# A hand-ordered list of operations is reordered: table load first, watches spread, count cast earlier

## The chip, the cores and the metric

The kernel runs on one core of a Trainium2 chip. The time is device microseconds of one execution, from which the median of three runs is shown; the profile is that of a further execution, with its own time. Engines: PE (TensorE: products), DVE (VectorE), ACT (ScalarE), POOL (GpSimd) and SP (SyncE, which only issues transfers here). Each engine works through its own list in order; a wait in it holds up all that is behind it.

## The reference

Two parts in a row. The first is a linear recurrence with complex gates, per batch (4), head (8) and step (768), with 48 x 48 states; the second is a feed-forward block with a squared ReLU on the 3072 tokens of 384 features that the first yields.

```python
mag = np.sqrt(a_re * a_re + a_im * a_im)
scale = np.minimum(mag, 0.999) / (mag + 1e-06)
a_re_n, a_im_n = (a_re * scale, a_im * scale)
for t in range(S):
    ar, ai = (a_re_n[:, :, t, :, None], a_im_n[:, :, t, :, None])
    new_re = ar * S_re - ai * S_im
    new_im = ar * S_im + ai * S_re
    S_re, S_im = (new_re + k_t * v_t, new_im)      # outer product
    y[:, :, t] = q_t @ S_re
x = y.transpose(0, 2, 1, 3).reshape(3072, 384)
h = np.maximum(x @ w_in, 0.0)                      # w_in 384 x 2048
out = h * h @ w_out                                # w_out 2048 x 384
```

The weights come as 8-byte floats and are decoded to 4-byte floats on the chip.

## The kernel before, in words

The tokens are worked in 12 groups (number gi) of two chunks (b = 0, 1) of 128 steps of one sequence each. For a group, the recurrence is turned into products of queries and keys that carry running products of the gates ("operands"), a masked score product per chunk, and a carried state. The feed-forward block then runs on the 256 tokens of the group.

The order of everything is written out by hand: FRONT is one string of tokens, `follow` walks through it and calls for each token the function that issues its instructions, and `manual_schedule` keeps that order on all five engines. The order of two tokens matters only if they have instructions on the same engine. Waits between engines and for transfers follow from the data. The tokens:

- l, i: loads of raw (the inputs of a group; l on SP's queue, ScalarE's and some on POOL, i on POOL for the first groups), v: values, f, j: transfers of words (a block of weights; f on SP, j on POOL). raw is one buffer for all groups.
- p0.k, q0.k: step k of the operands of group 0, chunk 0 and chunk 1; p1, q1: those of group 1; o2.k to o11.k: of later groups, both chunks at once. Steps 0 to 2, 4 to 6, 8 to 10, 12, 14, 18 and 22 are ScalarE's; 3, 7, 11, 13, 15, 16, 19, 20 and 23 to 30 VectorE's (of p0.9, too). 15, 23, 24, 25, 16, 26, 27 are seven steps that build running products in blocks (`steps_in_blocks`, two instructions each), 17 is the scan of the blocks' totals (`totals`, line 918: on POOL for group 0, on VectorE else), 18 copies it (`carries`, line 937), 19 multiplies it in (`carried`), 20, 28, 29, 30 are the four products of queries and keys, 21 two small transfers on SP (line 968).
- a, b: chunk 0 and 1 of a group: .0 scores, .1 and .3 keys transposed, .2 and .4 copied, .5 masked (VectorE), .6 values summed (line 1059), .7 tokens copied to x (line 1071, ScalarE), .8 the state's product (line 1084), .9 the new state. g: gap transfers within x (line 1129, SP), without which no product can start.
- U, S, A: the decoding of a block of words: two casts on ScalarE (lines 666, 674) and one operation on VectorE (line 682). A0 to A7 are the blocks of w_in, A8 to A15 of w_out.
- F, H: a part of the first product (groups 0 and 1 by chunk: line 1137, 24 records each; others line 1153, 12 records each) and the squared ReLU behind it (two ACTIVATEs). h_ps has two buffers. T, E: the second product of groups 0 and 1 (line 1173) and its eviction (line 1116). Z, X, Y, Q, R: the second product of the later groups in seven half products of 16 records (line 1243), the sums on VectorE that they need, and the output's parts (R: lines 1116, 1119). s: stores on SP.
- I: keep_busy, two products of an identity into an unused PSUM tile (four records each, line 579), which compute nothing.
- M: constants. M9 makes ident and the seed of the mask on POOL, M1 the mask: two copies on ScalarE (line 611), a transpose on TensorE (line 614), two copies on ScalarE (line 617). M0 is a small ACTIVATE with the function that p0.4 and q0.4 use, into a place that is overwritten later.
- w, W: the range check reads the weights a second time: w is a transfer of 384 KB into a single buffer (line 694), W two short ACTIVATEs on it (lines 704, 705). K0 compares what was gathered, K1 sums it over partitions on TensorE (line 1372), K2 casts the count (line 1375). All engines then load the count (line 1456) and branch past a second path that serves other inputs (line 1457); with these inputs it isn't taken.

Before, M0 stands behind p0.2, M9 ahead of i0.1.1, M1 behind p0.18, sixteen I's ahead of M1; most w and W stand in the second half, K0 ahead of Z11.4 and K1, K2 behind the last product.

Of the kernel before, what the change touches and what calls it, by code (L numbers as in the profile page):

```python
# [23 lines left out]
I32 = mybir.dt.int32  # L24
I16 = mybir.dt.int16
U32 = mybir.dt.uint32
U8 = mybir.dt.uint8
F8 = mybir.dt.float8e5
# [401 lines left out]
def quotient_path(ctx, tc, feat, vtok, w_in, w_out, w1, w2, out, n_seq, count):  # L430
# [816 lines left out]
    def outputs(i, r):  # L1247
# [242 lines left out]
```

## Time and profile before

| | us |
|---|---|
| median of 3 runs (lowest, highest) | 651.23 (650.91, 651.72) |
| profiled execution: time, span | 649.98, 648.2 |
| PE busy, DVE busy, ACT busy, POOL busy | 614.3, 480.2, 431.9, 72.9 |
| mean granted clock of TensorE | 0.988 of full speed |

The span is from the first to the last instruction of the profiled execution; its own time is 1.8 us longer. A busy PE is modelled and includes waiting of pipelined products, so its idle time says more than its busy time. The trace has all 6467 products of the program.

### The profile page before, as it was taken

The page shows a single profiled execution, that of the slowest core. Times are in us where ns is not written, and L with a number is a line of the kernel's source. Part 1 is how long each engine was busy: PE and PEld are TensorE (multiplying, and loading weights), DVE is VectorE, ACT ScalarE, POOL GpSimd, SP SyncE. Part 2 cuts the span into 40 slices and gives each one's busy share as a digit, 9 for nine tenths or more (in the row PEclk, how much of TensorE's full clock was granted, in tenths as well). Part 3 has the DMA queues.
Part 4 walks back from the last instruction along what each step waited for, and adds up shares of the span by engine and source line. Part 5 has one row for each costly group of instructions (what it writes and reads, how often), then busy time and mean ns, then how long its engine had stood idle before and what let it go on. Part 6 is the DMA issues. An engine that isn't in the chain of part 4 may idle for free.

```text
span 648.2 us, 15843 instructions
## 1 busy us (share of the span) xinstructions
PE 614.3 (95%) x6467; PEld 552.2 (85%) x6467; DVE 480.2 (74%) x937; ACT 431.9 (67%) x848; POOL 72.9 (11%) x154
## 2 busy tenths in 40 slices
PE   3389999999999999999999999999999999999994
PEld 3389977686899889889899898899899899889994
DVE  4889897887989878977969678877867958842040
ACT  5879998666677593784686785685685584653430
POOL 6662220010000010000030010001000001000000
PEclk9799999999999999999999999999999999999998
DMA  8889684261630620722555523743542530133101
GB/s 183 152 167 232 187 214 75 60 116 27 108 71 7 123 75 8 143 54 64 103 136 124 91 53 87 102 125 82 97 99 53 90 87 16 53 86 105 50 1 31
DMA packets 41883, 60.59 MB, mean 93 GB/s; under 512 B 6024, under 2 KB 30024, under 8 KB 41800
## 3 DMA queue, kind: packets, MB, share of 16 engines
q1 hardware_dynamic: 39624, 55.46, 39.3%
q0 software_dynamic: 1888, 3.69, 3.3%
q8 instruction: 53, 0.87, 0.6%
q10 hardware_dynamic: 288, 0.32, 0.2%
q14 instruction: 30, 0.25, 0.2%
HBM read 48.76 MB, written 4.72 MB: 83 GB/s over the span
## 4 chain that ended last, share of the span: by engine, by line
PE 84%; ACT 5%; DVE 4%; POOL 3%; DMA 2%; issue 1%; DVEq 0%; ACTq 0%; POOLq 0%
PE h_ps L1153 32%; PE o_ps L1243 28%; PE o_ps L1173 6%; PE a_ps L1022 4%; PE h_ps L1137 4%; PE y L1059 3%; PE y L1005 3%; PE turns L1084 2%; PE turns L1032 2%; DMA raw<-in_feat_dram 2%; POOL ab L918 1%; DVE pr L499 1%; POOL room L918 1%; DVE ab L499 1%; ACT room L823 0%
## 5 line engine op out<-in xcount | busy, mean ns | idle before, releaser
L1153 PE MATMUL h_ps<-x,w 128*128 128x256 f32 x960 | 212.6, 380 | 0.0
L1153 PEld LDWEIGHTS h_ps<-x,w 128*128 128x128 f32 x960 | 180.9, 190 | 24.2 <-DMA x<-x 0.2
L1243 PE MATMUL o_ps<-w,h 128*128 128x192 f32 x640 | 110.7, 329 | 0.0
L1243 PEld LDWEIGHTS o_ps<-w,h 128*128 128x128 f32 x640 | 103.7, 190 | 1.6 <-ACT o L1116 0.3
L1160 ACT ACTIVATE h<-h_ps 128x512 f32<-128x512 f32 x80 | 47.6, 595 | 75.6 <-PE h_ps L1153 70.0
L1243 PE MATMUL o_ps<-w_sum,mix 128*128 128x192 f32 x320 | 55.9, 330 | 0.7 <-DVE o L1119 0.7
L568 POOL COPY vt<-vt 64x192 f32<-64x192 f32 x48 | 28.0, 583 | 235.5 <-DMA vt<-in_vtok_dram 215.2
L1243 PEld LDWEIGHTS o_ps<-w_sum,mix 128*128 128x128 f32 x320 | 51.7, 190 | 1.7 <-DVE o L1119 1.0
L1161 ACT ACTIVATE h<-h 128x512 f32<-128x512 f32 x80 | 50.5, 631 | 2.5
L499 DVE TENSOR_TENSOR pr<-ab 128x384 f32<-128x384 f32 (+1 forms) x98 | 49.1, 501 | 2.6 <-ACT ab L889 0.2
L499 DVE TENSOR_TENSOR mix<-h 128x256 f32<-128x256 f32 x40 | 17.1, 427 | 41.7 <-ACT h L1161 41.6
L499 DVE TENSOR_TENSOR qk<-ab,qk 128x768 f32<-128x768 f32 (+1 forms) x56 | 46.5, 848 | 1.4
L499 DVE TENSOR_TENSOR room<-ab,carry 128x1344 f32<-128x1344 f32 (+1 forms) x28 | 36.9, 1360 | 11.5 <-ACT carry L937 11.3
L1137 PE MATMUL h_ps<-x,w 128*128 128x128 f32 x384 | 44.8, 276 | 0.0
L1173 PE MATMUL o_ps<-w,h 128*128 128x384 f32 x128 | 44.0, 489 | 0.7 <-ACT o L1116 0.7
L1137 PEld LDWEIGHTS h_ps<-x,w 128*128 128x128 f32 x384 | 43.7, 192 | 0.8
L808 ACT ACTIVATE ab<-raw 128x768 f32<-128x768 f32 (+1 forms) x28 | 37.1, 1376 | 1.7 <-DVE qk L499 1.6
L1071 ACT COPY x<-y 64x256 f32<-64x256 f32 (+1 forms) x72 | 26.5, 368 | 17.5 <-PE y L1059 16.5
L808 ACT ACTIVATE room<-z 128x768 f32<-128x768 f32 (+1 forms) x27 | 36.1, 1400 | 2.2 <-DVE z L855 2.2
L1022 PE MATMUL a_ps<-qk 48*64 48x64 f32 (+1 forms) x1152 | 37.4, 244 | 0.0
L1022 PEld LDWEIGHTS a_ps<-qk 48*64 48x64 f32 x1152 | 35.9, 133 | 0.7 <-issue 0.5
L1173 PEld LDWEIGHTS o_ps<-w,h 128*128 128x128 f32 x128 | 23.2, 190 | 14.3 <-ACT o L1116 0.8
(115 smaller groups left out, 994.0 us busy)
## 6 DMA issues: line engine op xcount, KB each, us to landing
raw<-in_feat_dram SPq DMA_DIRECT2D x40, 288.0 KB
words<-in_moe_w_out_dram SPq DMA_DIRECT2D x8, 768.0 KB
again<-in_moe_w_in_dram SPq DMA_DIRECT2D x16, 384.0 KB
again<-in_moe_w_out_dram SPq DMA_DIRECT2D x16, 384.0 KB
last<-qk SPq DMA_DIRECT2D x48, 97.5 KB
words<-in_moe_w_in_dram SPq DMA_DIRECT2D x8, 576.0 KB
vt<-in_vtok_dram SPq DMA_DIRECT2D x48, 96.0 KB
out_dram<-o SPq DMA_DIRECT2D x23, 192.0 KB
```

The costliest lines, as they stand in the source:

```text
L499: nc.vector.tensor_tensor(out=out, in0=in0, in1=in1, op=op)
L568: nc.gpsimd.tensor_copy(out=v[half_rows(h), PAD + DM:PAD + DM + DM // 2].rearrange("t (a x) -> t a x", x=HH * D), in_=pairs[half_rows(1 - ...
L808: nc.scalar.activation(out=out.rearrange("p c j n -> p c n j"), func=AF.Copy, in_=in_.rearrange("p c (n j) -> p c n j", j=L), **kwargs)
L1005: nc.tensor.matmul(ys[p_ % 2][crossed(hh, p_), p_ // 2], lhsT=states[b][1 - c_seq % 2][rows(hh), c, columns(hh, PAD + p_ * D)], rhs=operan ...
L1022: nc.tensor.matmul(to[:, :, 2] if s else to[:, :, 0:2], lhsT=operand(2 + c, p_, rows(hh))[:, half_rows(s)], rhs=q_[:, :, 1] if s else q_, ...
L1071: nc.scalar.copy(out=x_of[gi][to, odd::2, b * C:(b + 1) * C], in_=tiles["y"][odd][of, 0:NP // 2])
L1137: nc.tensor.matmul(ps[:, j], lhsT=w1_blocks[:, k, g, at:at + P], rhs=x_of[i][:, g, b * C:(b + 1) * C], start=(g == 0), stop=(g == NG - 1))
L1153: nc.tensor.matmul(ps[:, j], lhsT=w1_blocks[:, k, g, at:at + P], rhs=x_of[i][:, g], start=(g == 0), stop=(g == NG - 1))
L1160: nc.scalar.activation(out=h, in_=h_ps[i, f], func=AF.Relu, scale=of_w1)
L1161: nc.scalar.activation(out=h, in_=h, func=AF.Square)
L1173: nc.tensor.matmul(o_of[i, b], lhsT=tokens_of(i, f, b)[:, j], rhs=w2[:, k], start=(k == 0), stop=(k == NFB - 1))
L1243: nc.tensor.matmul(to, lhsT=x(k)[:, j], rhs=factor(z)[:, 2 * k + j], start=(z in (0, 1, 3) and k == j == 0), stop=(k == KH // 2 - 1 and j ...
```

## The change

Only the string FRONT changes. Both lists hold the same tokens, but for eight more keep_busy calls (I40 to I47) in the new one, and nearly every token's place is another. What the changed places are, as far as engines share them:

- M0 follows the first loads and stands ahead of p0.0. p0.5 stands ahead of p0.2, q0.0 ahead of p0.8.
- M9 stands behind i0.1.1; M1 stands ahead of p0.18 (behind it before), with 28 I's ahead of it. q0.15, q0.23, q0.24 stand ahead of p0.19 (behind p0.30 before), A3 behind a0.5, and I36 to I47 between a0.8 and F0.1.0. p1.25, A6, p1.16 stand behind b0.5 (ahead of it before).
- E0.0 stands ahead of o2.4.
- The 32 pairs of w and W are spread between o2.22 and H10.0. K0 stands among the sums of group 10, K1 among the first products of group 11, K2 ahead of Z11.5. Ahead of 300 us of products there are now some ten more watches.
- The order of transfers on SP and on POOL, as far as the first product, is the same in both lists.

```diff
 FRONT = (
-    "M6 M10 M2 l0.0.0 l0.0.1 j1 p0.0 p0.3 p0.4 p0.2 M0 p0.5 j0 p0.7 i0.1.0 p0.1 p0.8 M3 M4 "
-    "M5 q0.1 p0.10 p0.9 p0.11 p0.12 p0.15 p0.23 p0.24 l0.1.1 p0.25 q0.0 p0.22 q0.2 p0.16 "
-    "p0.26 p0.27 f1 U1 S1 q0.3 q0.4 q0.5 f0 l0.1.0 U0 S0 M7 A1 q0.7 q0.8 q0.9 q0.10 p0.13 j3 "
-    "A0 M9 i0.1.1 p0.14 v0.0 f3 f2 p0.6 p0.17 p0.18 q0.11 p0.19 I0 I1 I2 I3 I4 I5 I6 I7 I8 "
-    "I9 I10 I11 I12 I13 I14 I15 M1 U3 S3 p0.20 q0.22 l1.2.0 p0.28 q0.12 p0.29 q0.6 p0.30 "
-    "p0.21 q0.15 q0.23 q0.24 f4 j2 i1.2.0 j4 I16 I17 I18 I19 I20 I21 I22 I23 a0.1 a0.0 U2 S2 "
-    "q0.25 q0.16 a0.2 A2 q0.26 a0.3 q0.27 q0.13 V0.0 j5 A3 a0.4 a0.5 q0.14 M8 U4 S4 I24 I25 "
-    "I26 I27 a0.6 a0.7 q0.17 q0.18 A4 q0.19 q0.28 q0.20 f5 U5 S5 p1.0 p1.6 p1.3 p1.4 p1.5 "
-    "l1.2.1 g0.0 f6 q0.29 q0.30 q0.21 p1.1 j6 p1.2 p1.7 p1.8 I28 I29 I30 I31 I32 I33 I34 I35 "
-    "I36 I37 a0.8 p1.10 p1.9 j7 i1.2.1 f7 v0.1 I38 I39 F0.1.0 H0.1.0 U6 A5 F0.2.0 f8 a0.9 "
-    "V0.1 b0.1 p1.11 p1.12 p1.15 S6 p1.22 b0.0 p1.23 p1.24 p1.25 A6 b0.2 p1.16 H0.2.0 F0.0.0 "
-    "b0.3 b0.5 U7 S7 q1.0 b0.6 b0.7 H0.0.0 f9 g0.1 v1 b0.4 p1.13 U8 S8 A7 F0.3.0 H0.3.0 q1.3 "
-    "p1.26 p1.27 p1.17 p1.18 A8 p1.14 p1.19 p1.28 p1.20 p1.29 b0.8 p1.30 F0.3.1 H0.3.1 f11 "
...
-    "Y10.2 Z10.1 b11.0 X10.0 w26 Q10.3 Q10.1 Y10.0 Z10.2 R10.1 R10.2 Z10.3 R10.3 b11.5 b11.6 "
-    "W26 w24 Q10.2 Z10.4 Q10.0 Z10.5 b11.7 g11 F11.2 W24 w25 W25 H11.2 R10.4 R10.5 Z10.6 "
-    "F11.0 R10.6 H11.0 F11.4 H11.4 F11.1 F11.3 w30 H11.1 H11.3 Z11.0 F11.6 F11.5 H11.6 H11.5 "
-    "s10.1 s10.0 F11.7 X11.2 X11.0 H11.7 Y11.0 X11.1 Y11.2 Y11.1 Z11.1 Q11.2 R11.0 R11.1 "
-    "X11.3 Y11.3 Q11.3 Z11.2 Q11.1 R11.2 Z11.3 W30 K0 Z11.4 Q11.0 R11.3 Z11.5 R11.4 R11.5 "
-    "Z11.6 K1 K2 s11.2 R11.6 s11.0 s11.1")
+    "l0.0.0 l0.0.1 M0 M6 M10 p0.0 j1 p0.3 p0.4 p0.5 p0.2 M2 p0.7 p0.9 q0.0 j0 i0.1.0 q0.3 "
+    "p0.8 p0.1 l0.1.1 f1 f0 p0.10 p0.11 p0.12 M3 q0.4 q0.5 q0.1 M4 p0.15 l0.1.0 j3 p0.22 "
+    "q0.2 p0.23 p0.24 p0.25 p0.16 p0.26 p0.27 M5 U1 S1 U0 q0.7 q0.9 i0.1.1 S0 M7 A1 v0.0 "
+    "q0.8 f3 q0.10 p0.13 q0.11 A0 f2 M9 q0.12 p0.14 p0.6 q0.15 q0.23 q0.24 I0 I1 I2 I3 I4 I5 "
+    "I6 I7 I8 I9 I10 I11 I12 I13 I14 I15 I16 I17 I18 I19 I20 I21 I22 I23 I24 I25 I26 I27 M1 "
+    "p0.17 p0.18 p0.19 p0.20 p0.28 p0.29 p0.30 q0.22 U3 S3 I28 I29 I30 I31 I32 I33 a0.1 "
+    "l1.2.0 p0.21 f4 j2 U2 S2 q0.25 a0.2 q0.16 V0.0 i1.2.0 p1.6 A2 j4 j5 f5 q0.26 q0.27 I34 "
+    "a0.3 q0.13 a0.4 q0.6 a0.0 a0.5 I35 a0.6 q0.17 A3 M8 q0.14 U4 S4 a0.7 l1.2.1 g0.0 f6 "
+    "q0.18 A4 U5 S5 q0.19 q0.20 p1.0 q0.28 p1.3 p1.4 p1.5 q0.29 q0.30 q0.21 j6 j7 p1.1 p1.2 "
+    "a0.8 i1.2.1 f7 p1.7 p1.9 v0.1 p1.8 U6 p1.10 I36 I37 I38 I39 I40 I41 I42 I43 I44 I45 I46 "
+    "I47 F0.1.0 H0.1.0 A5 F0.2.0 a0.9 V0.1 p1.11 p1.12 p1.15 p1.23 q1.0 S6 p1.24 b0.1 b0.2 "
+    "q1.3 b0.0 F0.0.0 H0.2.0 b0.5 A6 U7 S7 p1.22 b0.6 b0.7 p1.25 p1.16 H0.0.0 b0.3 b0.4 f8 "
+    "f9 p1.26 U8 g0.1 S8 A7 F0.3.0 H0.3.0 p1.27 p1.17 v1 b0.8 p1.18 p1.13 F0.3.1 F0.2.1 A8 "
...
+    "R10.0 X10.1 X10.3 X10.2 Y10.3 a11.0 Z10.1 Y10.2 b10.8 a11.5 Y10.1 X10.0 Y10.0 K0 Q10.1 "
+    "a11.6 Z10.2 Q10.2 b10.9 a11.7 b11.0 R10.1 R10.2 Z10.3 b11.5 b11.6 Q10.3 b11.7 Q10.0 "
+    "R10.3 Z10.4 R10.4 Z10.5 R10.5 g11 F11.2 Z10.6 H11.2 F11.0 R10.6 s10.1 H11.0 F11.4 H11.4 "
+    "F11.1 F11.3 H11.1 H11.3 Z11.0 F11.6 H11.6 X11.2 Y11.2 X11.0 Y11.0 F11.5 F11.7 R11.0 K1 "
+    "H11.5 X11.1 H11.7 Y11.1 Z11.1 Q11.1 s10.0 X11.3 Y11.3 Z11.2 Q11.2 Z11.3 R11.1 R11.2 "
+    "Q11.0 Q11.3 Z11.4 R11.3 R11.4 K2 Z11.5 s11.2 R11.5 s11.0 Z11.6 R11.6 s11.1")
```

## Rows read from the trace of the kernel before

**Rows 1.** the page's part 4: shares of the chain that ended last, by engine

```profile
PE 84%; ACT 5%; DVE 4%; POOL 3%; DMA 2%; issue 1%; DVEq 0%; ACTq 0%; POOLq 0%
```

**Rows 2.** windows: length, busy us (instructions) per engine, TensorE clock, DMA share, GB/s

```profile
30.40:35.00 4.60, 4.60 (x22) 4.52 (x22) 4.39 (x9) 4.34 (x10) 3.88 (x8) 0.50 1.07 164
...
60.00:70.00 10.00, 9.40 (x130) 8.87 (x128) 9.55 (x29) 9.55 (x21) 1.18 (x4) 1.00 0.55 173
...
100.00:120.00 20.00, 19.31 (x189) 12.66 (x187) 15.41 (x20) 16.11 (x22) 1.15 (x2) 1.00 0.18 38
...
sum 589.00, PE 586.98 PEld 526.12 DVE 443.93 ACT 397.22 POOL 39.10; mean PE 53.36 PEld 47.83 DVE 40.36 ACT 36.11 POOL 3.55
```

**Rows 3.** timeline, 6 to 17 us: start, us, engine, line, operation [idle before, releaser]

```profile
6.33 1.28 ACT L823 ACT_TABLE_LOAD   x1 [6.33 <-DMA raw<-in_feat_dram]
...
8.48 1.28 ACT L842 ACT_TABLE_LOAD   x1
...
9.78 0.52 ACT L842 ACTIVATE z<-room 128x384 f32<-128x384 f32 x1
...
15.94 0.36 DVE L499 TENSOR_TENSOR pr<-ab 128x192 f32<-128x192 f32 x1
...
16.62 0.36 DVE L499 TENSOR_TENSOR pr<-ab 128x192 f32<-128x192 f32 x1
```

**Rows 4.** timeline of POOL, 10 to 29 us

```profile
10.40 0.22 POOL masks.py:197 MEMSET ident<- 128x128 f32 x1
...
15.66 0.51 POOL L537 DMA_DIRECT2D raw<-in_feat_dram  x1 [0.42 <-DMA words<-in_moe_w_in_dram]
...
28.62 0.43 POOL L918 TENSOR_TENSOR ab<-room 128x24 f32<-128x24 f32 x2
```

**Rows 5.** timeline, 11 to 31 us: fillers, the mask's transpose, p0.18, p0.19

```profile
11.04 9.23 PE L579 MATMUL idle<-ident 128*128 128x128 f32 x64 [11.04 <-POOL ident masks.py:199]
...
29.09 0.27 ACT L937 COPY carry<-ab 128x90 f32<-128x90 f32 x1 [1.52 <-POOL ab L918]
...
29.38 1.63 DVE L499 TENSOR_TENSOR room<-ab,carry 128x672 f32<-128x672 f32 x2 [1.20 <-ACT carry L937]
...
30.19 0.36 PE L614 MATMUL turns<-ident,plain 64*128 64x64 f32 x1 [9.91 <-ACT plain L611]
...
30.49 6.16 PE L579 MATMUL idle<-ident 128*128 128x128 f32 x32
```

**Rows 6.** timeline, 31 to 51 us: VectorE, ScalarE and the first product

```profile
31.93 2.25 DVE L499 TENSOR_TENSOR qk<-ab,qk 128x384 f32<-128x384 f32 x4
...
42.04 0.94 DVE L499 TENSOR_TENSOR a<-a_ps,mask 128x768 f32<-128x768 f32 x1
...
43.98 1.15 ACT L1071 COPY x<-y 128x256 f32<-128x256 f32 x3
...
50.38 5.52 PE L1137 MATMUL h_ps<-x,w 128*128 128x128 f32 x48
```

**Rows 7.** timeline, 64 to 79 us: decode A7, four products

```profile
64.10 0.95 DVE L682 SCALAR_TENSOR_TENSOR w<-words,part 128x768 int32<-128x768 int32 x1
...
67.55 10.98 PE L1137 MATMUL h_ps<-x,w 128*128 128x128 f32 x96
```

**Rows 8.** the chain that ended last, in order of time: start, us, what

```profile
107.26 0.64 ACT z L842
...
623.28 15.61 PE o_ps L1243 x96
```

**Rows 9.** waits: us in total, times, longest us

```profile
ACT size L704 <- DMA again<-in_moe_w_out_dram: 6.5, 3, 2.7
```

**Rows 10.** lines 1457 and 1486, sequencers: ns min/median/max, first to last start us

```profile
L1457 POOLq EVENT_SEMAPHORE  x1: 17/17/17, 643.6 to 643.6; - x1
...
L1486 POOLq DRAIN  x3: 40/107/3663, 643.7 to 647.9; - x3
...
L1486 SPq DRAIN  x3: 7/7/13, 645.5 to 647.6; - x3
```

136 rows, old and new, of the table FRONT are left out of this document.

## The prediction

> **What bounds the kernel now.** I read the page first: the chain that ended last runs on TensorE for 84% of the 648.2 us of span [rows 1]. Then the windows: from 50 us to 639 us TensorE stands idle for 2.0 us in all, 0.6 of it between 60 and 70 us and 0.7 between 100 and 120 [rows 2]. The products behind 50.38 us, where the first h_ps product starts (F0.1.0, [rows 6]), are the same in both lists, so whatever the order does to them it can give back at most some 2 us. What is left to gain lies ahead of F0.1.0 and behind the last product. Third, the timeline of the first 50 us, which is a race between engines and not a TensorE stretch [rows 3 to 6]. Last, the waits and the single lines of the end [rows 9, 10].
>
> **Table load.** M0 now runs while ScalarE waits for the first raw tile. The two loads of 1.28 us at 6.33 and 8.48 both stood in front of the first steps of operand set p0 [rows 3]; one is gone, the other hidden. The first puts p0.0 forward by 1.28. The second lay beside VectorE's p0.3 for the time that p0.3 took and stood alone for the rest, 0.7: p0.4 comes at 7.8 instead of 9.78, 2.0 us earlier. Behind it p0.2 now follows p0.5 and q0.0 precedes p0.8, two ScalarE steps of like size, which cancels. The first of the seven block steps (p0.15) comes at 14.0 instead of 15.94. The Trainium skill (ScalarE: Activation LUTs, "What ACT_TABLE_LOAD costs") adds a drain of 1380 ns to each load, 2.66 us together; the trace shows none, since the ACTIVATE at 9.78 follows the load of 8.48 at once [rows 3]. By the page two loads would cost 5.3 us, and by the rows 2.56.
>
> **What the lead meets.** The scan of totals p0.17 on POOL then ends at about 27.2 instead of 29.06 [rows 4]. But two operations changed places. M9 (ident and the mask's seed, on POOL) stood ahead of i0.1.1 and now stands behind it. The three transfers of i0.1.1 wait for earlier transfers of words and end at 15.66 + 0.51 = 16.17 [rows 4]; SP's and POOL's other transfers keep their order, so these waits stay. M9, begun at 10.40 with ident ready 0.64 later (the first filler product at 11.04, [rows 5]), will begin at 16.17, and ident is ready at 16.8. Second, 28 calls of keep_busy (112 records) now stand ahead of M1's transpose instead of 16 (64). At the fast pace of 0.112 (48 h_ps records in 5.52, [rows 6]) 112 take 12.5; the run of 64 took 9.23 where that pace makes 7.2, the run of 32 took 6.16 where it makes 3.6, with 0.275 of modelled tail in each, so the slow start adds 1.8 to 2.4 [rows 5]; in the second run the granted clock is 0.50, the lower of the two levels (1.2 GHz), after 10 us without a product [rows 2]. M1's transpose comes at 31.2 to 31.7, against 30.19. And M1 now stands ahead of p0.18 on ScalarE (it stood behind it): p0.18, ready at 27.2, waits for the copies of the mask until 0.6 behind the transpose, about 32.1, against 29.09 [rows 5]. So at p0.18 a lead of 1.9 has become a delay of 3.0, with bounds of 2.7 and 3.2 from the two slow starts. Queued behind it are all of ScalarE's list, and VectorE's p0.19.
>
> **What absorbs it.** p0.19 starts 0.3 behind p0.18, at 32.4, and from its start to the end of p0.30 it was 34.18 - 29.38 = 4.8 [rows 5, 6], so p0.30 ends at 37.2. From there to a0.5 it was 42.04 - 34.18 = 7.9. Of that stretch q0.15, q0.23 and q0.24 are done by now (three block steps of 16.62 - 15.94 = 0.68, [rows 3]; VectorE has 3.4 us to spare for them ahead of p0.19), and A3 (0.95, as A7 in [rows 7]) now follows a0.5: 4.9 is left, and a0.5 starts at 42.1 instead of 42.04. Between a0.5 and F0.1.0 both lists have a0.6, a0.8 and twelve calls of keep_busy (one more stands ahead of a0.6, hidden while a0.5 runs), so on TensorE's own path F0.1.0 comes at 50.4 to 50.5. The other path is ScalarE's: q0.13 used to end ahead of A3 at about 41.15 and now ends just ahead of a0.5, and q0.14, U4, S4 and the token copies a0.7 follow it. a0.7, at 43.98 before [rows 6], comes 0.9 later by that, and up to 3.0 later if the words that U4 reads decide it, since they are fetched behind p0.21. The gap transfers g0.0 follow a0.7; before, their data was there by 50.38, with a margin that no row gives. The ends for F0.1.0 are therefore +0.1 and +3.0; I take +0.6, near the first, because the margin and the words' own slack come off the second.
>
> Then VectorE, 9.5 us busy of ten, is the tightest [rows 2]. p0.18's delay reaches it again through q0.18 and q0.19, 1.0 later than before. On ScalarE U6, p1.10 and H0.1.0 now stand ahead of p1.12 (before U6 followed H0.1.0), so that VectorE waits 0.9 for p1.12 ahead of p1.15. b0.5 gets its time back, since p1.25, A6 and p1.16 moved behind it, but A7, which ended at 65.05 [rows 7], has p1.25, p1.16 and p1.26 ahead of it and ends at about 66.8, and the second half of F0.3.0 waits a good 1.0 for it. The row of four products that started at 67.55 [rows 7] starts at about 69.1. I take **+1.6** for the whole front (bounds 0 and +3).
>
> **The other parts.** o2.4 used to run (0.64, [rows 8]) ahead of the eviction E0.0 for which TensorE stood still behind 107.4 (the 0.7 idle of [rows 2]); now it follows E0.0, and the front is late itself: **-0.8** (bounds -0.9 and 0). Eight more keep_busy calls cost nothing elsewhere than told above. The watches (384 KB each by SP, two short ACTIVATEs) move from mostly behind 300 us to about one per 13 us between 90 and 520 us, by the products that stand between them in the list; ScalarE has room there (16.1 of 20 us between 100 and 120, [rows 2]), so their work is hidden; three of them waited 6.5 us for data before, at no cost that TensorE shows [rows 9]. I take 0 for the middle (bounds -1.2, the rest of the idle time, and +3).
>
> **The end.** The count was cast behind the last product, at about 639, and every engine loads it and branches past the second path. POOL, idle for long, came out of that at 643.6, then drained for 3.66 us until 647.3, last of all; SP, with the last store ahead of its load, was through at 645.6 [rows 10]. With the cast ahead of the last two products (2.6 us each, 96 records of six products in 15.61, [rows 8]) POOL does all this some 5 us earlier, and SP sets the end: 647.3 - 645.6, **-1.7** (bounds 0, if the drain waits for something else, and -2.0).
>
> Sum: +1.6 - 0.8 + 0 - 1.7 = -0.9 us, against 648.2 of span and 649.98 of that execution's time. The median of the runs shown is 651.23; the difference carried over gives **650.3 us**. This kernel's measurement can tell about 0.2%, 1.3 us, from no change.
>
> **Rivals.** *The front is absorbed.* Only TensorE's path counts and g0.0's data has margin; the row of products starts at 67.7. Then +0.2 - 0.8 - 1.7: 648.9. For it: on TensorE's path F0.1.0 is on time. Against: A7.
> *Ident is not late.* If i0.1.1 doesn't hold POOL up, M1 is through at 26, VectorE is free for p0.19 at 28.6, and F0.1.0 comes 3.8 earlier (0.8 there, 2.05 and A3's 0.95 behind): 3.8 + 0.8 + 1.7 less, 644.9. Against: the three waits in [rows 4].
> *The drain doesn't move.* POOL's 3.66 us end by something later: 652.0, no change.
> *Watches hold up ScalarE (slower).* Each stands in ScalarE's list ahead of a squared ReLU; h_ps has two buffers and a first product of 2.6 us, of which 0.6 are the read that frees a buffer, so some 2.0 us of waiting are free and the rest stalls TensorE. The longest wait was 2.7 [rows 9], which with the watch's own 1.5 costs 2.2 each; from two such on the gains above are gone, and with the ten or so that moved ahead of 300 us one or two beyond the forecast's margin are conceivable: 650.3 + 3.3 = 653.6. For it: one of them now lies at 88 us, where ScalarE has little room. Against: none cost anything before.
>
> **How the numbers follow.** Forecast 0.45 (0.15 of it under 649.9 us, 0.25 within 0.2%, and 0.05 slower by the front's upper bound), front absorbed 0.20, ident not late 0.08, drain doesn't move 0.09 (no change), watches 0.18 (0.15 of it slower, 0.03 within). That makes faster 0.43, same 0.37 and slower 0.20. The range leaves out ident not late and half of the watches' case: 646.5 to 653.6. The forecast alone would be 649.0 to 651.7.
>
> **What would show it.** One table load, ahead of 6.3; ident's memset at 16.2; the transpose L614 at 31 to 32, with ScalarE idle ahead of its copies; p0.19 at 32.4; F0.1.0 at 50.4 to 52; 96 records at L1137 from about 69; no idle at L1173 near 108; POOL's drain ahead of 645. The prediction is wrong if the transpose comes before 28, if TensorE's idle time behind 70 us is over 4 us, or if the drain still ends last.

## The result, and the profile after

The new list takes 655.20 us (median of 20 runs, 652.77 to 658.90), that of before 651.13 beside it (20 runs): a ratio of 1.0062, 95% interval 1.0047 to 1.0078, or 4.0 us more. I had forecast 650.3 and 0.9 us less; 655.2 lies above my range, which ended at 653.6. The profiled execution took 655.39 with 653.7 of span.

I cut both traces at two events: F0.1.0, where the first h_ps product starts, and the start of the last record of the last o_ps product (called the last product below).

| | F0.1.0 | from there to the last product | from there to the end |
|---|---|---|---|
| before | 50.38 | 588.2 | 9.6 |
| new | 53.76 | 592.9 | 7.0 |
| difference | +3.4 | +4.7 | -2.6 |
| forecast | +0.6 (+1.6 at the row of four products) | -0.8 + 0 | -1.7 |

So the end gained more than forecast, the front lost more, and the products, for which I had put down a gain of 0.8, lost 4.7.

The front of the new kernel, by the timeline (start, us, engine, line, operation, idle before and releaser):

```profile
2.65 1.28 ACT L590 ACT_TABLE_LOAD   x1 [2.65 <-issue]
3.94 0.20 ACT L590 ACTIVATE sums<-tiny 128x1 f32<-128x1 f32 x1
...
13.15 0.36 DVE L499 TENSOR_TENSOR pr<-ab 128x192 f32<-128x192 f32 x1
...
16.11 0.22 POOL masks.py:197 MEMSET ident<- 128x128 f32 x1
...
32.02 0.27 PE L614 MATMUL turns<-ident,plain 64*128 64x64 f32 x1
32.33 0.39 ACT L617 COPY mask<-turns 128x64 f32<-128x64 f32 x2 [6.47 <-PE turns L614]
32.55 0.28 ACT L937 COPY carry<-ab 128x90 f32<-128x90 f32 x1
...
44.49 1.08 ACT L666 ACTIVATE part<-words 128x768 int16<-128x768 uint32 x1 [1.10 <-DMA words<-in_moe_w_in_dram]
...
46.35 1.14 ACT L1071 COPY x<-y 128x256 f32<-128x256 f32 x3
...
53.76 5.60 PE L1137 MATMUL h_ps<-x,w 128*128 128x128 f32 x48 [1.57 <-DMA x<-x]
```

The lead of the table load is there and is larger than forecast: the first block step at 13.15, against 15.94 in [rows 3]. The Trainium skill (ScalarE: Activation LUTs, "What ACT_TABLE_LOAD costs") adds a drain of 1380 ns to a load; here the ACTIVATE follows at 3.94, when the load of 2.65 ends, as before. Then it goes as described: ident at 16.11 (forecast 16.2; 10.40 in [rows 4]), ScalarE idle for 6.47 us until the transpose, and p0.18 behind the mask's copies at 32.55 (forecast 32.1; 29.09 in [rows 5]). The last three rows are those of [rows 6]: U4 waits for its words, the token copies a0.7 start 2.4 later, and TensorE waits 1.57 us for the gap transfer, which SP began to issue at 47.12. The chain that ended last, in order of time, has three pieces that count here (start, us, what):

```profile
37.84 0.55 SPq L968
...
39.16 5.22 DMA words<-in_moe_w_in_dram
...
454.52 4.14 DMA x<-x
```

The first is p0.21 on SP, the second the fetch for U4, which stands behind it. The third belongs to the products. Of those, the windows (length, busy us and instructions of PE, PEld, DVE, ACT, POOL, TensorE clock, DMA share, GB/s):

```profile
100.00:120.00 20.00, 20.00 (x241) 14.99 (x240) 15.59 (x26) 18.63 (x28) 1.04 (x4) 1.00 0.30 54
...
400.00:500.00 100.00, 96.93 (x1096) 88.56 (x1096) 79.71 (x145) 68.70 (x139) 4.28 (x12) 1.00 0.42 86
```

The idle 0.7 us between 100 and 120 us of [rows 2] are gone, but between 400 and 500 TensorE now stands idle for 3.07 us. In the kernel before it was busy throughout:

```profile
400.00:500.00 100.00, 100.00 (x1093) 91.97 (x1092) 76.78 (x144) 73.10 (x149) 5.09 (x14) 1.00 0.44 94
```

Behind 70 us TensorE's idle time is 5.6 us in all (1.4 before), which is over the 4 us that the prediction had named as the sign of being wrong. The timeline of the new kernel at the three largest stalls:

```profile
399.47 0.36 DVE L1119 SCALAR_TENSOR_TENSOR o<-o_ps,o 128x192 f32<-128x192 f32 x1 [1.60 <-PE o_ps L1243]
399.75 0.95 DVE L499 TENSOR_TENSOR a<-a_ps,mask 128x768 f32<-128x768 f32 x1
...
400.75 1.00 PE L1059 MATMUL y<-a,vt 64*64 64x128 f32 x32 [0.99 <-DVE a L499]
...
453.32 0.39 SPq L694 DMA_DIRECT2D again<-in_moe_w_out_dram  x1
453.80 1.35 SPq L1129 DMA_DIRECT2D x<-x  x2
...
458.74 1.53 PE L1153 MATMUL h_ps<-x,w 128*128 128x256 f32 x6 [1.45 <-DMA x<-x]
...
497.71 1.75 DVE L901 TENSOR_TENSOR_SCAN room<-room,begun 128x768 f32<-128x768 f32 x1
499.50 0.96 DVE L499 TENSOR_TENSOR raw<-raw,room 128x768 f32<-128x768 f32 x1
500.37 0.35 DVE L1119 SCALAR_TENSOR_TENSOR o<-o_ps,o 128x192 f32<-128x192 f32 x1
...
500.78 0.92 PE L1243 MATMUL o_ps<-w_sum,mix 128*128 128x192 f32 x4 [1.65 <-DVE o L1119]
```

Each can be read back into the list. At 400 VectorE's list has R6.1, an output sum that waits for Z6.3, ahead of b7.5, the mask that TensorE needs next. At 500 it has the scan and the product of o10.13 ahead of R8.1, which must read its tile before Z8.3 may begin. At 457 SP has a watch's transfer, w31, ahead of the gap transfer g8. Together these waits are 4.1 us (0.99, 1.45 and 1.65).

The end, by lines 1457 and 1486 (sequencers: ns min/median/max, first to last start):

```profile
L1457 SPq EVENT_SEMAPHORE  x8: 17/17/17, 651.4 to 652.0; - x8
...
L1457 SPq COMPARE_BRANCH  x1: 45/45/45, 648.0 to 648.0; - x1
...
L1486 POOLq DRAIN  x3: 40/107/3663, 646.0 to 653.4; - x3
L1486 SPq DRAIN  x3: 7/7/13, 652.8 to 653.1; - x3
```

POOL's 3.66 us start at 646.0 and end at 649.7, ahead of SP's drain at 652.8; in [rows 10] they ended last.

### The profile page after: what moved, and what is told of

Read it like the earlier page. It is cut to its first block, busy times and chain, and to the rows that moved or that the text cites. A ratio compares the mean times of both kernels' runs of the same rounds, so it can differ in the third digit from the quotient of the medians.

```text
span 653.7 us, 15917 instructions
## 1 busy us (share of the span) xinstructions
PE 620.1 (95%) x6499; PEld 556.9 (85%) x6499; DVE 481.6 (74%) x937; ACT 431.1 (66%) x847; POOL 76.2 (12%) x154
## 4 chain that ended last, share of the span: by engine, by line
PE 79%; DVE 7%; DMA 5%; ACT 4%; POOL 2%; issue 1%; SPq 0%; DVEq 0%; ACTq 0%; POOLq 0%
PE h_ps L1153 32%; PE o_ps L1243 25%; PE o_ps L1173 6%; PE a_ps L1022 4%; PE h_ps L1137 3%; PE y L1005 3%; DMA raw<-in_feat_dram 2%; PE y L1059 2%; PE turns L1084 2%; DVE pr L499 2%; PE turns L1032 2%; DMA words<-in_moe_w_out_dram 1%; DVE ab L499 1%; DVE room L901 1%; ACT part L674 1%
## 5 line engine op out<-in xcount | busy, mean ns | idle before, releaser
L1243 PEld LDWEIGHTS o_ps<-w,h 128*128 128x128 f32 x640 | 103.8, 190 | 1.4
L1160 ACT ACTIVATE h<-h_ps 128x512 f32<-128x512 f32 x80 | 47.7, 597 | 75.8 <-PE h_ps L1153 74.4
L579 PE MATMUL idle<-ident 128*128 128x128 f32 x200 | 26.9, 299 | 16.8 <-POOL ident masks.py:199 16.8
L499 DVE TENSOR_TENSOR mix<-h 128x256 f32<-128x256 f32 x40 | 17.2, 431 | 34.1 <-ACT h L1161 34.1
L579 PEld LDWEIGHTS idle<-ident 128*128 128x128 f32 x200 | 25.8, 212 | 17.1 <-POOL ident masks.py:199 16.8
L499 DVE TENSOR_TENSOR a<-a_ps,mask 128x768 f32<-128x768 f32 x24 | 22.9, 955 | 23.0 <-PE a_ps L1022 22.8
```

Of the source, the lines that this page charges most:

```text
L499: nc.vector.tensor_tensor(out=out, in0=in0, in1=in1, op=op)
L579: nc.tensor.matmul(idle, lhsT=ident, rhs=ident, start=True, stop=True)
L1160: nc.scalar.activation(out=h, in_=h_ps[i, f], func=AF.Relu, scale=of_w1)
L1243: nc.tensor.matmul(to, lhsT=x(k)[:, j], rhs=factor(z)[:, 2 * k + j], start=(z in (0, 1, 3) and k == j == 0), stop=(k == KH // 2 - 1 and j ...
```

## The experiments

All are other orders of the same string, but for the watches that e13 and e14 leave out and the eight added keep_busy calls, which go with the new front. In the diffs a minus stands at a stretch as it was and a plus at the same stretch as it is in the run. Each ratio is to the kernel before on the same chip, with its 95% interval. The last three columns are the cuts of the table above, in one profiled execution, which can lie some us off its kernel's median.

| run | median us | ratio (interval) | F0.1.0 | products | end |
|---|---|---|---|---|---|
| e1 front undone | 652.88 | 1.0028 (1.0016 to 1.0041) | 49.8 | 591.6 | 7.1 |
| e2 front alone | 653.08 | 1.0035 (1.0022 to 1.0047) | 52.4 | 589.1 | 9.5 |
| e3 ident early | 651.33 | 1.0015 (0.9990 to 1.0039) | 48.0 | 594.9 | 6.7 |
| e4 count alone | 647.66 | 0.9950 (0.9935 to 0.9964) | 49.7 | 588.4 | 6.5 |
| e5 best parts | 644.86 | 0.9907 (0.9886 to 0.9928) | 46.9 | 588.4 | 6.8 |
| e6 three waits | 651.56 | 1.0001 (0.9982 to 1.0021) | 52.2 | 588.9 | 7.2 |
| e7 watches as before | 678.10 | 1.0428 (1.0402 to 1.0455) | 53.1 | 616.4 | 6.7 |
| e8 mask behind carries | 652.61 | 1.0016 (0.9998 to 1.0034) | 51.1 | 592.0 | 6.9 |
| e9 eviction first | 645.88 | 0.9910 (0.9891 to 0.9930) | 47.8 | 588.5 | 6.6 |
| e10 table alone | 648.57 | 0.9958 (0.9942 to 0.9974) | 47.7 | 588.6 | 9.6 |
| e11 spread alone | 677.92 | 1.0399 (1.0377 to 1.0421) | 52.2 | 619.2 | 6.7 |
| e12 count last | 656.64 | 1.0083 (1.0057 to 1.0109) | 51.4 | 593.4 | 9.6 |
| e13 no watches | 653.00 | 1.0025 (1.0007 to 1.0043) | 53.4 | 591.2 | 6.7 |
| e14 before, no watches | 650.38 | 0.9986 (0.9971 to 1.0000) | 52.2 | 586.9 | 9.5 |
| e15 four moves | 646.81 | 0.9924 (0.9903 to 0.9945) | 49.1 | 592.1 | 6.7 |
| e16 watch behind gap | 653.74 | 1.0039 (1.0023 to 1.0054) | 52.0 | 591.2 | 7.0 |
| e17 two parts | 647.14 | 0.9934 (0.9910 to 0.9958) | 47.6 | 588.2 | 6.6 |

**Which part loses (e1, e2).** Up to F0.1.0 the two lists hold the same tokens but for U6 and the keep_busy calls, so they can be cut there and crossed (U6 goes with the front and is kept once).

```diff
 e1: FRONT =
-  new list up to F0.1.0
+  list of before up to F0.1.0
   new list from F0.1.0 on
 e2: FRONT =
   new list up to F0.1.0
-  new list from F0.1.0 on
+  list of before from F0.1.0 on
```

> The list of before up to F0.1.0, the new list from there on. Theory: the front (first product at 53.76 instead of 50.38), the stretch of products behind it and the end each have their own price, +3.4, about +3.3 and -2.6 us against before. Then F0.1.0 is back at 50.4 and the time is before's 651.1 + 3.3 - 2.6 = 651.8. Rival: the products lose only because everything reaches them late from the front; then they lose nothing here and the time is 651.1 - 2.6 = 648.5.

> The new list up to F0.1.0, the list of before from there on. Theory (each part has its own price): F0.1.0 at 53.7 and the time 651.1 + 3.4 = 654.5. Rival (the late front carries the loss of the products): 651.1 + 3.4 + 3.3 = 657.8. Second rival (the slack behind the front takes part of it up): under 653.

The excesses of 0.28% and 0.35% add up to 0.63%, the whole of 0.62%: two prices of their own. The new front alone costs 2.3 us (1.4 to 3.1), of 3.4 that I had expected from F0.1.0 in one profile. The new rest costs 1.8 (1.0 to 2.7) though its end is 2.5 shorter: so the products lose some 4. With the front of before the new list's stalls of TensorE stand there too (0.99, 1.05 and 1.65 us at 396, 453 and 495); they are not a result of the late front.

**Why the front is late (e3, e8, e10).**

```diff
 e3, new list
+... M9 i0.1.1 ...
-... i0.1.1 S0 M7 A1 v0.0 q0.8 f3 q0.10 p0.13 q0.11 A0 f2 M9 ...
 e8, new list
-... I27 M1 p0.17 p0.18 p0.19 ...
+... I27 p0.17 p0.18 M1 p0.19 ...
 e10, list of before
-M6 M10 M2 l0.0.0 l0.0.1 j1 p0.0 p0.3 p0.4 p0.2 M0 ...
+M6 M10 M2 l0.0.0 l0.0.1 M0 j1 p0.0 p0.3 p0.4 p0.2 ...
```

> The new list with M9 alone moved back ahead of i0.1.1. Theory (the late identity is the front's loss): ident at about 11, the transpose for the mask at 26 to 27, p0.18 at 27.5, F0.1.0 at 49 to 50.4, and the time 655.2 - 3.4 to -4.5, about 651. Rival (the words of U4, 44.49 us, or TensorE's lower clock from 40 us set the front): F0.1.0 stays within 1 us of 53.8 and the time within 1 us of 655.2.

> The new list with M1 moved behind p0.18, as before; M9 stays late. Theory (the late identity reaches the rest only through M1's copies, which stand ahead of p0.18 on ScalarE): p0.18 at 27.5 to 28.5 instead of 32.55, F0.1.0 some 3 us earlier than 53.76, the time 2 to 3 less than 655.2. Rival (the late identity holds up the front by TensorE's own late start and low clock): F0.1.0 within 1 us of 53.8, time as new.

> The list of before with M0 alone moved behind l0.0.1. Theory: one load of 1.28 us instead of two, p0.15 at about 14.0 instead of 15.94 and p0.18 at about 27.2 instead of 29.09; of the 1.9 about 1 is left at F0.1.0 and at the end: 650. Rival (the transfers and POOL's scan set p0.18 and the front, so the lead is lost): F0.1.0 at 49.7 to 50.4, 651.3.

Each of the two moves takes back 3.0 us, 0.47% (e3; by the two intervals 1.2 to 4.9 us) and 0.46% (e8; 1.4 to 4.6), and in e8 ident is as late as in the new list. The timeline of e8:

```profile
27.35 0.27 ACT L937 COPY carry<-ab 128x90 f32<-128x90 f32 x1 [1.37 <-POOL ab L918]
...
32.52 0.40 ACT L617 COPY mask<-turns 128x64 f32<-128x64 f32 x2 [4.12 <-PE turns L614]
```

The mask's copies still come at 32.5; p0.18, now ahead of them, comes at 27.35. So the late ident costs the front its time through M1, which holds up p0.18 on ScalarE. By time, ident late with M1 behind p0.18 (e8) and ident early (e3) can't be told apart; that a late ident costs nothing else is not shown, since F0.1.0 is still 3.1 later in e8 than in e3 (51.1 and 48.0, one profile each). In e3 F0.1.0 comes 5.8 us earlier than in the new profile, yet the time falls by 3.0 and the products of that profile took 594.9, 2.0 more than in the new one: 1.1 of that is a wait of a1.0, 1.54 us there and 0.45 in the new profile, and the rest smaller waits. e15, below, shows on what a1.0 waits. In e10 the table load alone brings 2.7 us (1.7 to 3.8), more than the 1.4 that I had expected; its timeline:

```profile
2.65 1.28 ACT L590 ACT_TABLE_LOAD   x1 [2.65 <-issue]
...
18.12 0.56 POOL L918 TENSOR_TENSOR room<-ab 128x96 f32<-128x96 f32 x1 [2.07 <-DVE ab L499]
...
26.35 0.27 ACT L937 COPY carry<-ab 128x90 f32<-128x90 f32 x1 [1.50 <-POOL ab L918]
```

p0.18 comes at 26.35 instead of 29.09, 2.7 earlier, and F0.1.0 (47.7 instead of 50.4) and the time are earlier by the same 2.7.

**Why the products lose (e6, e13 to e16, e7, e11).**

```diff
 e6, new list
-... R6.1 s5.1 b7.5 ...
+... b7.5 R6.1 s5.1 ...
-... o10.13 V9.1 b9.6 b9.7 R8.2 s7.1 o10.12 o10.14 R8.1 ...
+... R8.1 o10.13 V9.1 b9.6 b9.7 R8.2 s7.1 o10.12 o10.14 ...
-... v10 V10.0 w31 o9.25 Q7.3 o9.13 o9.16 b8.7 g8 ...
+... o9.25 Q7.3 o9.13 o9.16 b8.7 g8 v10 V10.0 w31 ...
 e15: e6 with M9 ahead of i0.1.1; e16: new list with w31 alone behind g8
 e13, e14: new list and list of before without w0 to w31 and W0 to W31
 e7: new list, each w and W ahead of the neighbour on its engine that it has before (K0, K1 around Z11.4)
 e11: e4 (below), each w and W behind the product that it has ahead of it in the new list
```

> The new list with three local moves: b7.5 ahead of R6.1 (VectorE), R8.1 ahead of o10.13 (VectorE), and g8 ahead of v10 and w31 (SP). Theory: the three stalls of TensorE at 400 (1.15), 457 (1.6) and 500 (1.7) are waits of the new list and vanish, 4.4 less at the last product: about 650.8. Rival (the stalls are where TensorE's lead over another engine runs out, and come back a little later): 654 or more, with stalls of like size behind these places.

> The new list with M9 ahead of i0.1.1 and the three local moves (b7.5 ahead of R6.1, R8.1 ahead of o10.13, g8 ahead of v10 and w31). Theory (the two causes add up): 655.2 - 3.9 - 3.6 = 647.7. Rival (a common limit, VectorE's or ScalarE's whole work, takes one of them back): 649.5 or more.

> The new list with w31 alone moved behind g8. Theory (of the stall at 457 us w31 is only its own issue, 0.4 to 0.5, and v10's last transfers are the rest): the stall is 0.5 shorter, 654.7. Rival (w31 is the whole of it): the stall is gone, 653.6.

> The new list without the 32 pairs w and W: the weights are not read a second time, and that part of the range check is left out. Theory (the three stalls are waits on VectorE's and SP's order, in which only w31 has a hand): the stalls at 400 (1.15) and 500 us (1.72) stay, the one at 457 loses 0.4 or more; 653.5 to 655. Rival (the spread watches are what the products of the new list lose): 651 to 652, stalls gone.

> The list of before without the 32 pairs w and W, so without the second reading of the weights. Theory (watches are hidden where the list was made around them): 650.5 to 651.3, the stall of 0.99 near 390 us stays. Rival (they cost something before too): 649 or less.

> The new list with the 32 pairs w and W put back ahead of the same neighbours on SP and ScalarE as before, and K0 to K2 set for that (K0 ahead of Z11.4, K1 behind it, K2 ahead of Z11.5). Theory (the watches are hidden wherever they stand; only w31 ahead of g8 costs 0.4): 654.2 to 655.2, the stalls at 400 and 500 us as they are. Rival (the spread watches are what the products lose): 651 to 652, the stalls gone.

> The list of before with K1 behind Z11.4 and K2 ahead of Z11.5, as in the run with the count alone, and besides with the 32 pairs w and W at the places that the new list gives them among the products. Theory (spread watches are hidden): 647.7, as with the count alone, and the stalls of TensorE as there. Rival (they hold up ScalarE, as watches did when they were put back by neighbours): over 650, with stalls behind waits for the second reading of the weights.

e6 takes back all 0.6%: the ratio is 1.0001, and from F0.1.0 to the last product it is 588.9, what the list of before takes (588.2 to 589.1 in the seven profiles with it and its watches in place). The windows of e6 (TensorE alone), where the new kernel's middle row had 96.93:

```profile
300.00:400.00 100.00, 99.64 (x1034) 1.00 0.46 94
400.00:500.00 100.00, 100.00 (x1092) 1.00 0.42 87
500.00:600.00 100.00, 100.00 (x1060) 1.00 0.27 55
```

The stalls don't come back later, so no other limit stands behind them there. With ident early as well (e15) the time is 646.81; the two causes add up (647.7 expected). The largest stall that is left there stands at 80 us, by its timeline:

```profile
80.24 0.32 PE L1005 MATMUL y<-last,state 48*64 48x128 f32 x1 [1.98 <-DMA last<-qk]
```

It is a wait of a1.0 for the small transfers of a step 21. All nine profiles with the new front and the new rest have it, 0.45 to 1.98 us, longest in the two with an early ident (1.54 in e3, 1.98 here); e1, with the front of before, has none.

On the watches my theory was wrong in a size. e16 moves w31 alone, and the whole stall at 457 us goes, not 0.5 of it. The timeline of e16:

```profile
451.58 1.42 SPq L1129 DMA_DIRECT2D x<-x  x2
453.05 0.57 SPq L694 DMA_DIRECT2D again<-in_moe_w_out_dram  x1
...
455.40 1.89 PE L1153 MATMUL h_ps<-x,w 128*128 128x256 f32 x8
```

From the issue of the gap transfers to the product that waits for them it is now 3.8 us at most (TensorE was busy until then, and in e13, without watches, too), and was 4.94 behind the 384 KB of w31. So at least 1.1 us of the delay were the transfer itself, and 0.5 the issue of w31 ahead of it. The size varies: in the five profiles with w31 ahead of g8 (new, e1, e3, e8, e12) it is 3.97 to 5.40 us, and the stall 0.47 to 1.90. The Trainium skill (DMA: Bandwidth & Descriptors, "Queues, rings and completion order") says that each DMA engine consumes the descriptors of a queue in ring order, though a later one may finish its write before an earlier one; by that the gap transfer's descriptors start behind those of w31, and the longer 3.97 to 5.40 us agree with it. Without any watch (e13) the new list gains 0.37%, 2.4 us; the list of before (e14) 0.14%, 0.9 us, at the edge of what can be told. The stalls at 400 and 500 stay in e13. By that the spread costs this list the difference of the two, 1.5 us, which is what w31 alone costs (e16: 0.23% less than new). Both are barely clear of the noise (the interval of the difference is -0.3 to 3.3 us, that of e16 0.1 to 2.9); the vanished stall is the firmer sign.

e7 and e11 missed by far what I had expected (655 and 647.7) and told nothing of that share, since both made new waits of their own. But they show that watches are hidden only in a list that was made around them: by the ratios e7 is 24 us over the new list, e11 29 us over e4. In e7 TensorE's largest stall is 12 us, for a gap transfer behind Z10.5. The waits of e11 (us in total, times, longest us):

```profile
PE y L1059 <- DMA vt<-in_vtok_dram: 4.9, 1, 4.9
PE h_ps L1153 <- ACT h L1160: 4.1, 1, 4.1
...
ACT room L823 <- DMA again<-in_moe_w_in_dram: 5.4, 1, 5.4
```

A w waits on SP until the last W has freed the one buffer (up to 4.3 us at line 694 in e11), and all of SP's list behind it waits too, here the loads of values and of inputs.

**The end (e4, e12).**

```diff
 e4, list of before
-... Z11.4 Q11.0 R11.3 Z11.5 R11.4 R11.5 Z11.6 K1 K2 s11.2 ...
+... Z11.4 K1 Q11.0 R11.3 K2 Z11.5 R11.4 R11.5 Z11.6 s11.2 ...
 e12, new list
-... R11.0 K1 H11.5 ... R11.4 K2 Z11.5 s11.2 R11.5 s11.0 Z11.6 R11.6 ...
+... R11.0 H11.5 ... R11.4 Z11.5 s11.2 R11.5 s11.0 Z11.6 K1 K2 R11.6 ...
```

> The list of before with K1 moved behind Z11.4 and K2 ahead of Z11.5, nothing else. Theory: POOL's drain of 3.66 us ends ahead of SP's, which sets the end; from the last product to the end of the span 7.0 us instead of 9.6, so 651.1 - 2.6 = 648.5. Rival (what is behind the last product is as long, since SP's last store, its branch and the code behind it come after the last product anyway): 650.5 to 651.1.

> The new list with K1 and K2 moved behind Z11.6, as before. Theory (POOL's drain of 3.66 us ends last again, and SP loads the count between its last store and its branch): from the last product to the end 9.6 instead of 7.0, the time 655.2 + 2.6 to 3.8 = 657.8 to 659. Rival: no change, 655.2.

By the profiles the end is 9.5 to 9.6 with the count last (five kernels) and 6.5 to 7.2 with the count moved (fourteen): 2.8 on average, with and without the rest of the change. By times e4 gives 3.3 (2.3 to 4.2); e12 lost only 1.4 against the new list, where 2.6 was expected; the intervals of the two ratios hold 2.6 as well, so the times of e12 leave the size open. In e12, by lines, POOL's drain is last again:

```profile
L1486 POOLq DRAIN  x3: 40/107/3663, 650.0 to 654.3; - x3
L1486 SPq DRAIN  x3: 7/7/13, 651.8 to 654.0; - x3
```

**Parts put together (e5, e9, e17).**

```diff
 e5: new list up to F0.1.0 with M9 ahead of i0.1.1, then e4 from F0.1.0 on
 e9: e5 with
-... o2.4 T0.5.0 T0.6.0 T0.7.0 E0.0 b1.0 ...
+... T0.5.0 T0.6.0 T0.7.0 E0.0 o2.4 b1.0 ...
 e17: e4 with M0 behind l0.0.1
```

> The new list up to F0.1.0 with M9 ahead of i0.1.1, the list of before from there on, with K1 behind Z11.4 and K2 ahead of Z11.5. Theory: the parts add up: the front with an early identity gains some 2 us at F0.1.0 against before (47.98 instead of 50.38) of which about 1 is left at the last product, the end gains 2.6 to 3.8 as when the count alone was moved: 646.5 to 648. Rival (the lead of the front is given back by VectorE before 110 us): the same time as with the count alone, 647.7, or up to 1 more.

> The list of the fastest run so far (new front with M9 ahead of i0.1.1, products of before, count moved ahead) with o2.4 moved behind E0.0. Theory (the eviction is what TensorE waits for near 105 us, 0.7 to 1.2 in the runs with the products of before): that stall vanishes and the time falls by 0.7, to about 644.2. Rival (VectorE or ScalarE makes TensorE wait a little later instead): 644.9, a new stall behind 105 us.

> The list of before with two parts of the change and nothing else: M0 behind l0.0.1, and K1 behind Z11.4, K2 ahead of Z11.5. Theory (the table load lies ahead of everything and the end behind it, so their gains, 2.7 and 3.2 us by the ratios of the runs alone, add up): 651.4 - 5.9 = 645.5. Rival (the lead of the front is given back among the products when the end is another): 647.5 or more.

e5 is the fastest kernel here: 644.86, 0.93% under before (0.72 to 1.14) and 1.5% under the new one (by the two ratios); I had expected 646.5 to 648. e17, with two of the change's parts alone, is 0.66% under (0.42 to 0.90); 645.5, the plain sum, would be 0.9%, at the interval's edge, so up to 1.6 us of the sum may be given back. e9 gained nothing that can be told (its ratio is that of e5 within 0.3%, so a gain of 0.8 us could hide there): the stall behind b1.0, 0.61 us at 105 in e5, is gone, and one of like size stands 13 us later, by its timeline:

```profile
117.48 2.20 PE L1173 MATMUL o_ps<-w,h 128*128 128x384 f32 x6 [0.48 <-ACT o L1116]
```

## Why the prediction was wrong, step by step

**The step that failed: "I take 0 for the middle (bounds -1.2 ..., and +3)", and the sentence ahead of it that the order behind 50.38 can give back at most some 2 us.** That sentence bounds a gain and says nothing of a loss. The products are the same, but nearly every token around them has another place, and I checked only the watches and E0.0. Measured from F0.1.0 to the last product, outside the bound of +3: +4.5 on average (592.9, 591.6, 594.9, 592.0 and 593.4 in the five profiles with the new rest and all its watches, against 588.2 to 589.1), of which three waits are 4.1, and e6 shows that moving five tokens takes all of it away. All three could have been read from the new list: who stands ahead of the operation that TensorE waits for, on VectorE and on SP, and what that waits for. The measured terms, +2.3 for the front, +4.5 for the products and -2.8 for the end, add up to the measured +4.0.

**E0.0 ahead of o2.4: -0.8, no gain shown.** The idle time near 107 went in the new list, as forecast, but in e9, which has this move by itself, one of 0.48 us came up at the next eviction and the time did not fall. With the old order the wait is no fixed price either: 0.28 us in e17, 0.69 before, 1.24 in e2. A stall that is one of several close limits was priced as if nothing stood behind it.

**Front: +1.6, measured +2.3 (1.4 to 3.1, e2); right in mechanism.** Ident behind i0.1.1 and M1 ahead of p0.18 are shown by e3 and e8: either move takes the loss away. That the sum came near is in part luck, since two terms were off and cancelled in part. The table load gives 2.7 to 2.8 at p0.15 and POOL's scan, not 1.9. And of the two ends for F0.1.0, +0.1 and +3.0, I chose +0.6, near the first; in the new profile the second path decides: p0.21 on SP, the words for U4, a0.7, the gap transfer. F0.1.0 comes at 51.4 to 53.8 in the seven profiles with the new front, 52.6 on average, and at 49.7 to 52.2 (50.8) in the five with that of before, +1.8; the last section says where the spread of the latter comes from. The extra 1.0 that I saw behind F0.1.0, by A7, didn't show: from F0.1.0 to the row of four products it is 17.3 in the new profile and 17.2 before. Where nothing stands in the way of the table load's lead (e10), it arrives whole.

**The end: -1.7, measured -2.8.** POOL's drain does move, and SP sets the end, as forecast. I left SP's own end where it was. But SP's load of the count stood between its last store and its branch; now it lies ahead of that store, and the branch comes 1.3 us behind the last product instead of 2.7 (648.0 and 646.7 in the new profile, 641.3 and 638.6 before). Of these 1.4 us 0.5 are lost again behind the branch.

**The rivals.** "The front is absorbed" did not hold (e2: +2.3), nor "The drain doesn't move" (POOL's drain starts at 646.0, ahead of the last product). "Ident is not late" did not hold either, since ident came at 16.11; e3 puts it early and takes back 3.0. "Watches hold up ScalarE" comes nearest in size (653.6), but by luck: the watches' share is one watch, on SP, 1.5 us, and the larger part of the loss is the two waits on VectorE's order.

## What to carry to other kernels

Price a re-ordered list from both sides: besides the waits that it removes, go through every operation that the bound engine waits for and ask what now stands ahead of it on its own engine, and what that in turn waits for; three such pairs cost 4.1 us here, more than the 2.8 that the new list gains at its end. Where one queue carries both, put a large transfer that nobody waits for (here the second reading of the weights) behind a small one that the bound engine needs, not ahead of it. And take a change of many parts to pieces: the table load (-2.7) and the early count (-3.3) were good by themselves and bring 4.3 us together (e17), so the rest of the same list cost some 8 us (4.0 + 4.3).

## What the runs showed that I had not expected

- A transfer of 384 KB issued 0.5 us ahead of the gap transfers on the same queue made them at least 1.1 us longer (4.94 from issue to product in the new profile, 3.97 to 5.40 in five, 3.8 at most without).
- POOL's drain takes 3.66 us wherever it stands (18 of the 19 profiles; 3.86 in e7), and SP's first instruction behind its branch comes 3.4 us later (648.0 to 651.4) in the new kernel and 2.9 before (641.3 to 644.2).
- TensorE's clock in the front of the new kernel, by its windows:

```profile
35.00:40.00 5.00, 2.16 (x20) 1.52 (x22) 4.79 (x11) 4.44 (x8) 0.00 (x0) 0.92 0.18 28
40.00:50.00 10.00, 10.00 (x162) 9.30 (x155) 7.33 (x16) 7.44 (x17) 9.32 (x22) 0.70 1.06 203
```

  After a stretch with 2.16 us busy of 5 the granted clock stands at 0.50 (the lower level, 1.2 GHz) from 40 to 46 us, and the 64 score records at 39.60 take 3.0 us from the first start to the last, where before, at full clock, they took 2.0. What that costs the end was not measured by itself.
- TensorE's clock also moves F0.1.0 between profiles of one and the same front. Up to F0.1.0 the lists of before and of e14 are the same; these are the 40 filler records at 44 us, first before, then e14:

```profile
43.87 4.73 PE L579 MATMUL idle<-ident 128*128 128x128 f32 x40
...
44.05 6.36 PE L579 MATMUL idle<-ident 128*128 128x128 f32 x40
```

  The granted clock between 44 and 48 us is 1.00 before and 0.55 to 0.60 in e14, the fillers take 1.6 us longer there, and F0.1.0 comes at 52.19 instead of 50.38. e11 goes as e14 does (6.36 us, 52.16). So a difference of 2 us at F0.1.0 between two single profiles can be the clock's and not the list's.
